# Hash-masked attention and a channel mix on one core: the fourth pair's values, three fillers, the last output's transpose and the order

## The chip, the core and the metric

The program runs on one core of a Trainium2 chip. The core has five engines with a queue of instructions each: PE (matmuls, with PEld for the loads of their stationary operand), ACT (exp, relu, tanh), DVE (vector work), POOL (more vector work) and SP, which here only issues DMAs. The metric is the time of one execution on the device in microseconds (us); less is better. The median of several executions is taken.

## The reference, cut to what matters

```python
q_bits = (einsum('bhsd,dk->bhsk', q, proj) > 0)          # 6 bits for each row; k_bits likewise
mask   = q_bucket[:, :, :, None] == k_bucket[:, :, None, :]
scores = where(mask, (q @ k.T) / sqrt(D), -1e9)
attn   = exp(scores - max);  attn /= (sum(attn) + 1e-9)
x      = (attn @ v)  laid out as (B, S, H * D)
x_prev = x shifted by one row (zeros ahead)
xk = mu_k * x + (1 - mu_k) * x_prev;   xr likewise with mu_r
out = sigmoid(xr @ w_r) * (relu(xk @ w_k) ** 2 @ w_v)
```

There are 4 batches, 8 heads, 768 rows, a head size of 64, a model size of 512 and an inner size of 1024. All inputs and the output are fp32.

## The kernel before

The heads are worked in 16 pairs, n = 0 to 15, four to a batch; behind a batch's last pair stands its channel mix (`add_moe`). For each pair:

- **Preparation.** q and k (`nat`) are split into a high and a low half of 64 columns each, both fp16, by DVE (L398 and L401, into `nh`), and turned by a DMA (L405) into `a`. Six more rows of `a` hold the hash bits: PE computes the projections (L427), DVE makes words of plus or minus a constant of their signs (L431, into `bx`), and POOL copies them into place with four instructions (L443, "the rows"), one for each of q and k and each head of the pair. With the bits as extra rows of the contraction, a score whose bits differ comes out so low that its exp vanishes, so there is no mask.
- **Scores.** Nine steps of 1024 columns: matmuls on PE (L544) into one of four PSUM buffers of two banks, then an exp on ACT (L548) into `pt`.
- **Values.** `pt` times the values `va` with a column of ones behind them, six groups of matmuls a pair (L571); DVE takes the reciprocal of the sums (`rc`) and multiplies (L589, into `ob`).
- **Rows without a partner.** A small share of the values' sum stands in for the mean. Pairs below `NUC` do it by a matmul (L566): POOL casts the values (L350), sums them together with the ones (L356, L359, L362, into `vsu`), and PE multiplies the sum by a matrix of 1e-12 (`tiny`) ahead of the pair's values. From pair `NUC` on, POOL sums the values alone (into `vs`), PE makes their mean in two layouts (L374 and L375, behind each other under the name mean), DVE subtracts it from the values (L380, two instructions a pair, into `va`) and keeps it by column (L387, into `mc`); the reciprocal then takes an add first (L584, L585 in place of L582), and the mean comes back at the mixing.
- **Turning the output.** `ob` is turned to `xt`, either on PE with six transposes (L599) and a copy by DVE (L602), for the pairs in `OT_PE`, or by a DMA that SP issues (L605). L612 makes its shifted neighbour; from pair `NUC` on, L609 writes the column ahead of the first row.
- **Mixing.** DVE takes the difference of neighbours (L630, `df`), and then, for `xk` and for `xr`, one instruction (L635) below `NUC`, two (L641, L644) from `NUC` on.

The channel mix of a batch multiplies `xk` by w_k (L659), takes the relu (ACT, L663) and the square (DVE, L666); multiplies `xr` by w_r (L679) and takes a tanh (ACT, L682); multiplies the squares by w_v (L692), and DVE combines the two (L699) for the store (L702). The weights are cast on POOL (L304). `warmb` ("fillers", L251) are pairs of matmuls on zeros, whose result nobody reads.

All of this is made as a list of operations, and a table, `ORDER`, gives the order in which they are issued, for all engines together; each engine takes its own in that order and waits for what the operation at its head needs. A second table, `BANKS`, gives each PSUM buffer its bank. So an operation that waits holds up everything behind it on its engine. Numbers behind a buffer's name tell its copies apart.

Of the kernel before, what the change touches and what calls it, by code (L numbers as in the profile page):

```python
# [128 lines left out]
def kernel(  # L129
# [30 lines left out]
    NUC = 4  # L160
# [6 lines left out]
    OT_PE = (0, 1, 2, 3, 15)  # L167
# [611 lines left out]
```

## Time and profile before

| | us |
|---|---|
| median of 3 runs | 243.16 (242.25 to 243.25) |
| the profiled execution | 242.0 |
| its span in the profile | 240.2 |
| PE busy | 234.1 |
| ACT busy | 181.9 |
| DVE busy | 179.8 |
| POOL busy | 99.7 |

The profile is of one execution. The span runs from its first instruction to its last; the profiled execution's own time is a little longer. "Busy" sums the instructions of an engine. PE and PEld overlap, and the ends of matmuls are modelled. In the rows of a timeline stand the start in us, the duration, the engine, the line, the operation and its tiles, and behind them, in brackets, how long the engine had been idle and what it waited for; x4 puts four in a row together.

### The profile page before, as it was taken

To read this page: it belongs to the slowest core of one execution; us is meant where nothing else is said; L and a number is where in the kernel's file an instruction comes from. 1 tells how busy PE (TensorE), PEld (TensorE's weight loads), DVE (VectorE), ACT (ScalarE), POOL (GpSimd) and SP (SyncE) were. 2 spreads that over 40 slices of the span, in tenths; PEclk is the share of its full clock that TensorE was granted. 3 is DMA by queue.
4 is the path that set the end of the run, shared out by engine and by line. 5 is a ranking of instruction groups with operands and counts; after the bars stand their busy time and mean duration, and the time that the engine had idled before them with its cause. 6 is when DMAs were issued, how large, how long until landed. Compare 5 with 4: busy or idle time off the path is not lost.

```text
span 240.2 us, 6251 instructions
## 1 busy us (share of the span) xinstructions
PE 234.1 (97%) x2515; PEld 147.8 (62%) x2532; DVE 179.8 (75%) x388; ACT 181.9 (76%) x242; POOL 99.7 (41%) x148
## 2 busy tenths in 40 slices
PE   8999999999999999999999999999999999999994
PEld 6985776776766565656456656665566564455442
DVE  3488789999998898989868896887167867348232
ACT  2699999999999999889779999677884640256320
POOL 4064979989934899438087302550000000000000
PEclk9999999999999999999999999999999999999999
DMA  6989999999999999988999989401500401210333
GB/s 225 304 222 274 232 242 260 279 197 362 279 253 284 273 213 294 249 302 206 276 163 241 249 177 234 136 0 26 173 0 3 120 3 44 87 46 1 131 135 131
DMA packets 72605, 44.00 MB, mean 183 GB/s; under 512 B 54912, under 2 KB 67584, under 8 KB 72576
## 3 DMA queue, kind: packets, MB, share of 16 engines
q1 hardware_dynamic: 72208, 43.20, 70.9%
q8 instruction: 20, 0.33, 0.6%
q10 hardware_dynamic: 368, 0.39, 0.5%
q14 instruction: 9, 0.07, 0.1%
HBM read 24.12 MB, written 6.29 MB: 127 GB/s over the span
## 4 chain that ended last, share of the span: by engine, by line
PE 92%; ACT 5%; issue 1%; DVE 0%
PE ps_all L544 25%; PE ps_all L692 17%; PE ps_all L659 16%; PE ps_all L571 14%; PE ps_all L679 8%; ACT pt L548 4%; PE ps_all L427 4%; PE ps_all L489 2%; PE ps_all L512 1%; PE ps_all L478 1%; ACT kr L663 1%; PE ps_all L251 1%; PE ps_all L246 1%; PE ps_all L599 1%; PE ps_all L566 1%
## 5 line engine op out<-in xcount | busy, mean ns | idle before, releaser
L548 ACT ACTIVATE pt<-ps_all 128x1024 bf16<-128x1024 f32 x144 | 138.4, 1041 | 10.9 <-PE ps_all L544 10.3
L544 PE MATMUL ps_all<-a 128*128 128x256 f16 (+1 forms) x384 | 79.2, 325 | 0.5 <-ACT pt L548 0.3
L443 POOL COPY a<-bx 6x384 f32<-6x384 f32 x56 | 38.9, 695 | 34.4 <-DVE bx L431 19.6
L544 PEld LDWEIGHTS <-a 128*128 128x128 f16 x384 | 34.0, 98 | 23.5 <-issue 4.6
L659 PE MATMUL ps_all<-xk,wk 128*128 128x384 bf16 x256 | 48.3, 326 | 0.1
L571 PEld LDWEIGHTS <-pt 128*128 128x128 bf16 x1152 | 42.5, 97 | 8.0 <-issue 0.5
L692 PE MATMUL ps_all<-wv,k 128*128 128x512 bf16 (+2 forms) x199 | 45.6, 362 | 0.5
L571 PE MATMUL ps_all<-va,pt 128*128 128x65 bf16 x1152 | 44.8, 193 | 0.0
L663 ACT ACTIVATE kr<-ps_all 128x384 bf16<-128x384 f32 x64 | 29.4, 491 | 16.0 <-PE ps_all L659 14.4
L659 PEld LDWEIGHTS <-wk 128*128 128x128 bf16 x256 | 24.2, 98 | 17.0 <-issue 0.6
L692 PEld LDWEIGHTS <-k 128*128 128x128 bf16 x208 | 19.3, 98 | 18.9 <-issue 0.3
L699 DVE SCALAR_TENSOR_TENSOR os<-rs,ps_all 128x512 f32<-128x512 f32 (+2 forms) x26 | 16.5, 643 | 19.0 <-PE ps_all L692 13.7
L682 ACT ACTIVATE rs<-ps_all 128x512 f32<-128x512 f32 x24 | 14.3, 602 | 20.5 <-PE ps_all L679 14.1
L666 DVE TENSOR_TENSOR k<-kr 128x384 bf16<-128x384 bf16 x64 | 23.2, 389 | 8.3 <-ACT kr L663 8.3
L401 DVE SCALAR_TENSOR_TENSOR nh<-nat,nh 128x1536 f16<-128x1536 f32 (+1 forms) x16 | 27.0, 1694 | 0.2
L679 PE MATMUL ps_all<-wr,xr 128*128 128x512 bf16 x88 | 23.2, 379 | 0.4
L356 POOL TENSOR_TENSOR vt<-vn 128x384 f32<-128x384 f32 x12 | 17.8, 1485 | 12.5 <-DMA vn<-in_v_dram 11.7
L589 DVE TENSOR_TENSOR ob<-ps_all,rc 128x384 bf16<-128x384 f32 x32 | 17.5, 553 | 1.4 <-DMA xt<-ob 0.8
L431 DVE TENSOR_SCALAR bx<-ps_all 128x768 uint16<-128x768 uint16 x14 | 13.4, 956 | 5.3 <-PE ps_all L427 4.7
L398 DVE TENSOR_SCALAR nh<-nat 128x1536 f16<-128x1536 f32 (+1 forms) x16 | 15.8, 985 | 0.3 <-PE ps_all L512 0.2
L679 PEld LDWEIGHTS <-xr 128*128 128x128 bf16 x96 | 9.0, 98 | 9.0
L380 DVE SCALAR_TENSOR_TENSOR va<-ps_all,vn 128x384 bf16<-128x384 f32 x24 | 12.7, 548 | 0.5 <-PE ps_all L375 0.2
(77 smaller groups left out, 188.9 us busy)
## 6 DMA issues: line engine op xcount, KB each, us to landing
vn<-in_v_dram SPq DMA_DIRECT2D x16, 384.0 KB, 5.1
out_dram<-os SPq DMA_DIRECT2D x23, 256.0 KB, 2.3
nat<-in_k_dram SPq DMA_DIRECT2D x15, 384.0 KB, 4.7
nat<-in_q_dram SPq DMA_DIRECT2D x15, 384.0 KB, 5.2
wst<-in_moe_w_k_dram SPq DMA_DIRECT2D x2, 512.0 KB, 7.0
wst<-in_moe_w_r_dram SPq DMA_DIRECT2D x2, 512.0 KB, 5.8
wst<-in_moe_w_v_dram SPq DMA_DIRECT2D x2, 512.0 KB, 4.4
k<-in_moe_w_k_dram SPq DMA_DIRECT2D x1, 512.0 KB, 4.4
```

Source lines behind the costliest of these rows:

```text
L356: e.tensor_tensor(out=vt[:, :, :, 0:E], in0=src[:, :, 0:3, 0:E], in1=src[:, :, 3:6, 0:E], op=ALU.add)
L401: nc.vector.scalar_tensor_tensor(out=nh[:, :, D:P], in0=nat.rearrange("p j (c d) -> p (j c) d", d=D), scalar=QS, in1=nh[:, :, 0:D], op0=AL ...
L443: nc.gpsimd.tensor_copy(side_a[side][n % NAQ][D : D + NB, j, :].bitcast(FP32), bx_t[sx][32 * i : 32 * i + NB, :].bitcast(FP32))
L544: nc.tensor.matmul(ps[:, lo - s * STEP : hi - s * STEP], side_a["k"][sa][:, j, jc * P : (jc + 1) * P], side_a["q"][sa][:, j, q0 : q0 + hi ...
L548: nc.scalar.activation(out=pt_t[sp][:, s * STEP : (s + 1) * STEP], in_=ps_t[plan.slot[nm]], func=AF.Exp, bias=EBIAS, scale=ESC)
L571: nc.tensor.matmul(oo[:, ic * 65 : ic * 65 + 65], pt_t[sp][:, o : o + P], va_t[sa][:, j, jc, 0 : D + 1], start=(not uc and ic == 0 and jc ...
L589: nc.vector.tensor_tensor(out=ob_t[so][:, :, j * D : (j + 1) * D], in0=oo[:, :, 0:D], in1=rc_t[sr][:, 1, :].unsqueeze(2).to_broadcast([P, ...
L659: nc.tensor.matmul(ps[:, 0:HALF], wk_sb[:, d, fc * P : (fc + 1) * P], xk_t[mx[d]][:, h * HALF : (h + 1) * HALF], start=(d == 0), stop=(d = ...
L663: nc.scalar.activation(out=kr_t[sk], in_=sm(nm)[:, 0:HALF], func=AF.Relu, scale=0.5 ** 0.5)
L666: nc.vector.tensor_tensor(out=k2_t[s2][:, h * HALF : (h + 1) * HALF], in0=kr_t[sk], in1=kr_t[sk], op=ALU.mult)
L679: nc.tensor.matmul(sm(nr), xr_t[mx[d]][:, c * P : (c + 1) * P], wr_sb[:, d, :], start=(d == 0), stop=(d == NDC - 1))
L692: nc.tensor.matmul(sm(nv)[:, x0:x1], k2_t[(b * NFC + fc) % NK2][:, c * P : (c + 1) * P], wv_sb[:, fc, x0:x1], start=(fc == 0), stop=(fc == ...
```

## The change

`NUC` goes from 4 to 3, so the fourth pair (n = 3) has its mean subtracted as the later pairs have. Five fillers are left of eight. Pair 15 is no longer in `OT_PE`, so its output is turned by a DMA. `ORDER` and `BANKS` are new tables.

```diff
 ORDER = [
...
-    0, 16, 2, 3, 4, 21, 5, 6, 7, 20, 8, 9, 10, 11, 37, 41, 33, 26, 1, 29, 28, 36, 30, 32, 40, 69, 72, 71, 70, 74, 73, 25, 43, 27, 31, 79,
...
+    0, 34, 66, 69, 38, 30, 23, 31, 16, 68, 71, 1, 26, 25, 2, 33, 3, 67, 70, 4, 27, 20, 29, 37, 74, 22, 5, 109, 6, 40, 24, 28, 7, 19, 44, 8,
...
 BANKS = [
-    2, 6, 2, 0, 4, 0, 0, 0, 0, 4, 4, 0, 3, 7, 1, 5, 4, 6, 1, 4, 5, 3, 4, 5, 2, 3, 4, 5, 4, 3, 0, 1, 2, 3, 0, 0, 0, 1, 7, 6, 6, 0, 2, 2, 2,
...
+    7, 5, 0, 0, 5, 6, 1, 2, 5, 0, 6, 1, 5, 1, 2, 4, 0, 0, 2, 7, 4, 6, 1, 2, 3, 2, 3, 2, 0, 3, 2, 0, 1, 1, 0, 5, 6, 6, 3, 1, 1, 2, 1, 0, 0,
...
-    NUC = 4
+    NUC = 3
...
-    OT_PE = (0, 1, 2, 3, 15)
+    OT_PE = (0, 1, 2, 3)
...
-    for i in range(8):
+    for i in range(5):
         def filler(i=i):
             for _ in range(2):
                 nc.tensor.matmul(sm(f"warmb{i}")[:, 0:256], wz[:, 0:P], wz[:, 0:256], start=True, stop=True)
```

On DVE, from the bits of pair 4 (`bx_67`) to those of pair 5 (`bx_68`), before:

```order
L431 TENSOR_SCALAR bx_67<-ps_all 128x768
L398 TENSOR_SCALAR nh_61<-nat_58 128x24x64
L630 TENSOR_TENSOR df_101<-xt_95 128x768
L401 SCALAR_TENSOR_TENSOR nh_61<-nat_58,nh_61 128x24x64
L582 RECIPROCAL rc_89<-ps_all 128x6
L589 TENSOR_TENSOR ob_92<-ps_all,rc_89 128x6x64
L582 RECIPROCAL rc_91<-ps_all 128x6
L589 TENSOR_TENSOR ob_93<-ps_all,rc_91 128x6x64
L635 SCALAR_TENSOR_TENSOR xr_111<-df_101,mur,xt_95 128x768
L602 COPY xt_96<-ps_all 128x768
L431 TENSOR_SCALAR bx_68<-ps_all 128x768
```

And the first half of the same place in the new order; `va_78` are the values of the fourth pair, and behind the last row shown stand eleven more ahead of `bx_68`: L585, L612, L589, two `va` of the next pair, `xr`, L584 and L585, `xk`, L589 and `mc`:

```order
L398 TENSOR_SCALAR nh_61<-nat_58 128x24x64
L431 TENSOR_SCALAR bx_67<-ps_all 128x768
L612 COPY xt_95<-xt_95 128x127
L380 SCALAR_TENSOR_TENSOR va_78<-ps_all,vn_69 128x6x64
L630 TENSOR_TENSOR df_101<-xt_95 128x768
L380 SCALAR_TENSOR_TENSOR va_78<-ps_all,vn_69 128x6x64
L582 RECIPROCAL rc_89<-ps_all 128x6
L387 TENSOR_SCALAR mc_84<-ps_all 128x1
L589 TENSOR_TENSOR ob_92<-ps_all,rc_89 128x6x64
L401 SCALAR_TENSOR_TENSOR nh_61<-nat_58,nh_61 128x24x64
L602 COPY xt_96<-ps_all 128x768
L584 TENSOR_SCALAR rc_91<-ps_all 128x6
```

One instruction, L398, has moved from behind the first bits to ahead of them, and 21 stand between the two bits where there were nine.

On POOL, from the rows of pair 3 (`a_66`) to the sums of pair 5, the new order (+) against the old (-); the first three sums taken away and put in are those of the fourth pair, and `a_64` are the rows of pair 5:

```order
 L443 COPY a_66<-bx_68 6x384 x4
-L356 TENSOR_TENSOR vt_72<-va_78 128x390
-L359 TENSOR_TENSOR vt_72<-vt_72 128x2x65
-L362 TENSOR_TENSOR vsu_76<-vt_72 128x130
+L356 TENSOR_TENSOR vt_72<-vn_69 128x6x64
+L359 TENSOR_TENSOR vt_72<-vt_72 128x2x64
+L362 TENSOR_TENSOR vs_74<-vt_72 128x128
 L356 TENSOR_TENSOR vt_72<-vn_70 128x6x64
 L443 COPY a_63<-bx_67 6x384 x4
```

The fourth pair's sums stay where they were, ahead of the rows of pair 4 (`a_63`), and take the values in fp32.

On SP, the last DMAs, before:

```order
L605 DMA_TRANSPOSE xt_94<-ob_92 128x6x128
L702 DMA out_dram<-os 128x512 x3
L605 DMA_TRANSPOSE xt_96<-ob_92 128x6x128
L702 DMA out_dram<-os 128x512 x13
L702 DMA out_dram<-os 128x128 x2
L702 DMA out_dram<-os 128x256
```

And in the new order, where `xt_97<-ob_93` is the output of pair 15:

```order
L605 DMA_TRANSPOSE xt_96<-ob_92 128x6x128
L702 DMA out_dram<-os 128x512 x3
L605 DMA_TRANSPOSE xt_97<-ob_93 128x6x128
L702 DMA out_dram<-os 128x512 x10
L702 DMA out_dram<-os 128x128 x2
L702 DMA out_dram<-os 128x512
L702 DMA out_dram<-os 128x256
```

The added DMA stands behind three stores, and one full store has moved to between the two small ones and the last.

116 rows, old and new, of tables (BANKS, ORDER) are left out of this document.

## The prediction

> **What bounds the kernel now.** The page first, for the share of each engine:
>
> ```profile
> span 240.2 us, 6251 instructions
> PE 234.1 (97%) x2515; PEld 147.8 (62%) x2532; DVE 179.8 (75%) x388; ACT 181.9 (76%) x242; POOL 99.7 (41%) x148
> ```
>
> The profiled execution took 242.0 us, 1.8 us more than its span; the median of the runs is 243.16 us, 1.16 us above it. I make the sum against 242.0 and carry that difference over to the median. A measurement of this kernel can tell about 0.5% from no change, 1.2 us.
>
> PE's 97% is an average, and its ends are modelled, so the next view is busy time by stage (the stretch, its length, then PE, PEld, DVE, ACT and POOL, each with its count):
>
> ```profile
> 20.00:45.00 25.00, 24.98 (x398) 17.37 (x396) 22.50 (x33) 25.00 (x29) 19.55 (x24) 1.00 1.08 258
> 45.00:58.00 13.00, 12.99 (x206) 8.76 (x203) 12.49 (x30) 12.79 (x15) 11.82 (x15) 1.00 1.13 271
> 58.00:85.00 27.00, 26.63 (x310) 17.08 (x309) 24.99 (x50) 26.51 (x39) 18.42 (x20) 1.00 1.14 281
> 120.00:200.00 80.00, 79.47 (x833) 48.23 (x842) 58.62 (x149) 59.85 (x80) 20.20 (x32) 1.00 0.49 115
> ```
>
> Two kernels in one. From 20 to 85 us ACT is idle for 0.7 us of 65 (25.00 + 12.79 + 26.51 busy), with DVE at 22.50 of 25 and 12.49 of 13 beside it: the exps pace this part, and PE is busy because its work is let in between them. From 120 us on ACT has 20 us to spare in 80 and PE 0.53: the matmuls pace that part. So a microsecond of PE work is worth a microsecond only well behind 85 us; ahead of that, what counts is whether the next exp finds its scores ready. The view of waits says the same: from 58 to 85 us ACT waited for the scores once.
>
> ```profile
> ACT pt L548 <- PE ps_all L544: 0.4, 1, 0.4
> ```
>
> **The change part by part.** *Fillers.* The head keeps five in both versions; the three that go stood in the middle of the scores. The timeline shows the first and the last of them, each with the weight load that follows:
>
> ```profile
> 26.84 0.21 PEld L251 LDWEIGHTS <-k 128*128 128x128 bf16 x2
> 27.06 0.51 PEld L571 LDWEIGHTS <-pt 128*128 128x128 bf16 x12
> ...
> 35.67 0.31 PEld L251 LDWEIGHTS <-k 128*128 128x128 bf16 x2
> 35.99 0.32 PEld L544 LDWEIGHTS <-a 128*128 128x128 f16 x3
> ```
>
> From a filler's start to the next work's is 0.22 and 0.32 us, so three are 0.7 to 1.0 us of PE. All lie where ACT was busy for 25.00 of 25.00: I count 0, and 0.9 in a rival.
>
> *Fourth pair.* What goes (the first three rows) and what comes, as groups with the mean of one in ns:
>
> ```profile
> L566 PE MATMUL ps_all<-vsu,tiny 128*128 128x390 bf16 x8 | 2.6, 330 | 0.0
> L350 POOL CAST va<-vn 128x768 bf16<-128x768 f32 x4 | 4.1, 1060 | 7.7 <-DMA vn<-in_v_dram 7.7
> L635 DVE SCALAR_TENSOR_TENSOR xk<-df,muk,xt 128x768 bf16<-128x768 bf16 x4 | 4.5, 1135 | 0.0
> L374 PE MATMUL ps_all<-vs,ones 128*128 128x128 bf16 x12 | 2.6, 220 | 0.0
> L380 DVE SCALAR_TENSOR_TENSOR va<-ps_all,vn 128x384 bf16<-128x384 f32 x24 | 12.7, 548 | 0.5 <-PE ps_all L375 0.2 <-issue 0.2
> L387 DVE TENSOR_SCALAR mc<-ps_all 128x1 f32<-128x1 f32 x12 | 1.7, 142 | 0.0
> L584 DVE TENSOR_SCALAR rc<-ps_all 128x6 f32<-128x6 f32 x24 | 3.8, 157 | 10.0 <-PE ps_all L571 9.5 <-ACT pt L548 0.6
> L641 DVE TENSOR_SCALAR tm<-df,muk,mc 128x768 f16<-128x768 bf16 x12 | 5.6, 470 | 0.1
> L644 DVE TENSOR_TENSOR xk<-tm,xt 128x768 bf16<-128x768 f16 x12 | 6.6, 553 | 0.1
> ```
>
> DVE gains 2 x 0.55 (va), 0.14 (mc), 0.14 (xz, another one-column instruction) and 2 x 0.16 (the adds of rc), 1.7 us, and loses 2 x (1.13 - 0.47 - 0.55) = 0.2: **+1.5 us on DVE**, nearly all ahead of 60 us. DVE was idle for 2.5 + 0.5 us from 20 to 58, so the work fits if it comes at the right places; I price it with the order below. POOL loses a cast of 1.06 us and gets wider sums for it, in an engine that is busy for 19.55 of 25: 0. PE loses two matmuls of 0.33 and gains one of 0.22 and a smaller one, at most 0.4 less, in the part that ACT paces: 0.
>
> There is a new wait. The fourth pair's sums (L362 ends them) now feed a matmul (L374) that stands in PE's queue right behind the fourth pair's bits (L427), with scores and the values' matmuls queued behind it.
>
> ```profile
> 39.64 0.83 PE L427 MATMUL ps_all<-a,p 128*32 128x512 f16 x16
> 39.93 0.42 POOL L362 TENSOR_TENSOR vsu<-vt 128x130 bf16<-128x130 f32 x1
> ```
>
> The sums ended at 40.35 us and those bits at 40.47, so PE finds them just ready: 0 to 0.5 us of PE, under ACT's stock of waiting scores, so 0 for the sum.
>
> *New order, pair 5.* Here I expect the cost. The rows of DVE, POOL and ACT around the bits of pair 4 (the first L431) and of pair 5 (the second), and two groups:
>
> ```profile
> 41.09 0.95 DVE L431 TENSOR_SCALAR bx<-ps_all 128x768 uint16<-128x768 uint16 x1
> 42.82 0.86 DVE L630 TENSOR_TENSOR df<-xt 128x768 bf16<-128x768 bf16 x1
> 42.15 4.41 POOL L443 COPY a<-bx 6x384 f32<-6x384 f32 x4
> 43.60 2.05 DVE L401 SCALAR_TENSOR_TENSOR nh<-nat,nh 128x1536 f16<-128x1536 f32 x1
> 47.89 0.55 DVE L602 COPY xt<-ps_all 128x768 bf16<-128x768 bf16 x1
> 48.81 0.96 DVE L431 TENSOR_SCALAR bx<-ps_all 128x768 uint16<-128x768 uint16 x1 [0.37 <-PE ps_all L427]
> 49.78 0.55 DVE L380 SCALAR_TENSOR_TENSOR va<-ps_all,vn 128x384 bf16<-128x384 f32 x1
> 49.89 2.40 POOL L443 COPY a<-bx 6x384 f32<-6x384 f32 x4 [0.57 <-POOL vt L356]
> 54.31 3.77 ACT L548 ACTIVATE pt<-ps_all 128x1024 bf16<-128x1024 f32 x4 [0.21 <-PE ps_all L544]
> L589 DVE TENSOR_TENSOR ob<-ps_all,rc 128x384 bf16<-128x384 f32 x32 | 17.5, 553 | 1.4 <-DMA xt<-ob 0.8
> L612 DVE COPY xt<-xt 128x127 bf16<-128x127 bf16 x16 | 3.5, 221 | 0.1
> ```
>
> Before, the second L431 began 7.72 us behind the first (48.81 - 41.09), 0.37 of it idle, so 7.35 us of work. In the new order L398 has gone ahead of the first, and between the two stand 21 instructions: 4 va, 3 ob, 5 of rc, df, lo, xt, xr, xk, 2 xs, 2 mc. By the rows: 4 x 0.55 + 3 x 0.55 + 5 x 0.16 + 0.86 + 2.05 + 0.55 + 2 x 1.13 + 2 x 0.22 + 2 x 0.14 = 11.1 us, and 12.0 with the first L431 itself. Instructions in a row start closer than they last (L431 to L380 above 0.97, but L630 to L401 0.78 for 0.86), which takes off some 6%: 11.3 us, **3.6 us more** than before, or 4.3 without that discount.
>
> The cover: the rows of pair 5 ended at 52.29 us (49.89 + 2.40) and its first exp began at 54.31, 2.0 us later, of which I give 0.7 to a score step and its hand-over. That leaves 1.3 us. And the new order asks first for a score step that needs two of the four rows only, 2 x 0.6 = 1.2 us more. Cover 2.5, delay 3.6: ACT waits **1.1 us**, with 0 and 2.3 as ends (none if the first L431 comes that much earlier than before, 2.3 if all four rows are needed after all).
>
> Does the added DVE work also hold up POOL's rows? Four of them took 2.40 us from 49.89 on while a `va` ran, and 4.41 us from 42.15 on beside L630 and L401. So I count the added `va` on DVE alone. Three POOL instructions more (two sums and a cast, about 1 us each by L350) now stand ahead of pair 5's rows; they run while the second L431 is late, so they cost nothing beyond that. [...]
>
> *Last output by a DMA.* Six transposes go from PE, in the part that PE paces. The weight loads of the last output's six and of the work behind them; the landing of DMA transposes in general; and two rows of the chain for the price of a group of matmuls:
>
> ```profile
> 201.35 0.54 PEld L599 LDWEIGHTS <-ob 128*128 128x128 bf16 x6
> 201.85 0.58 PEld L679 LDWEIGHTS <-xr 128*128 128x128 bf16 x4
> DMA to landing us min/median/max: 2.7/4.1/8.6
> 208.97 3.25 PE ps_all L659 x20
> 229.09 5.18 PE ps_all L692 x24
> ```
>
> From their first weight load to the next work's is **0.50 us**. [...] Is the landing covered? Behind the last matmul of pair 15 the new order has one L659 group (3.25 / 5 = 0.65 us) and ten of L692 or L679 (5.18 / 6 = 0.86 each), 9.3 us, before the last batch's first matmul on this output. The chain needs rc and ob (1 us), the landing, and xs, df, tm, xk with two L699 between (some 3.5 us): 7.2 us with the shortest landing, 8.6 with the median. On SP, only stores that are ready stand ahead of it. So it is covered: 0. If a landing took the longest, 8.6 us, the chain would be 13.1 and the cost 3.8.
>
> *The tail.* A full store now stands just ahead of the last one.
>
> ```profile
> out_dram<-os SPq DMA_DIRECT2D x23, 256.0 KB, 2.3
> ```
>
> It lands 2.3 us after its issue, and the last one is issued a matmul group behind it, so I count 0.
>
> **Sum:** -0.5 (transposes) + 1.1 (pair 5) = +0.6 us: 242.6 us profiled, 243.8 us as a median.
>
> **Rivals.** *A, PE's work counts everywhere.* If PE and ACT pace the first 85 us together, as 24.98 of 25.00 for PE lets one think, each filler is time: -0.9 for them, -0.4 for the fourth pair's matmuls, -0.5 for the transposes, and no wait at pair 5 because the scores get ahead: -1.8, and with ACT's 0.7 us of gaps -2.5 at most. 240.2 us profiled, 241.4 as a median (down to 240.7). For it: three of the four edits take work from the busiest engine. Against: ACT's 25.00.
>
> *B, pair 5 late in full.* The bank of PSUM that the fifth pair's bits leave is next taken by a matmul (L374) that stands ahead of more groups and the pair's first scores in PE's queue, so if the second L431 is late, PE stops too, and the stock of scores runs dry; with PE behind, the -0.5 is lost as well. Without the discount the delay is 4.3 and the wait 1.8. Pair 4 has the same pattern: its first exp comes one exp earlier in ACT's order, and a row beside DVE work took 1.1 us (4.41 / 4), so up to 1.1 for it. Price 1.1 to 3.4, typically +1.8: 243.8 us profiled, 245.0 as a median. It decides from a delay of the second L431 of over 4.2 us: 1.7 us of wait, 1.2 with the transposes off.
>
> [...]
>
> **How the numbers follow.** The forecast 0.33, A 0.32, B 0.33, C 0.02. Faster by over 0.5% is A, 0.32; within 0.5% is the forecast and C, 0.35; slower is B, 0.33. The likeliest case alone runs from 242.2 (no wait at pair 5, and half of the fillers counted) to 244.4. The range goes down to A, 240.8, and up to 245.6, which takes in two thirds of B.
>
> **What would show it.** Right: L431 of pair 5 starts at 51.5 us or later, ACT has a gap of 0.5 to 1.5 us before the first exp of pair 5, and from 85 us on PE has no new gap and six transposes fewer. A is right if ACT's counts up to 58 us (29 and 15) rise by one or more. B is right if ACT's busy time from 45 to 58 falls by over 1.5 us from 12.79. Wrong altogether would be a wait for `xt<-ob` before the last batch, or a gain or loss of over 1 us that arises behind 120 us.

## The result, and the profile after

| | before | after | ratio (95% interval) |
|---|---|---|---|
| median, us | 242.72 (17 runs) | 244.23 (17 runs) | 1.0059 (1.0044 to 1.0073) |
| the profiled execution, us | 242.0 | 243.6 | |
| its span, us | 240.2 | 241.7 | |

The change makes the kernel 1.5 us, or 0.6%, slower. The prediction was a median of 243.8 us, 0.6 us more than the one it started from, and it put its likeliest case within 0.5%. The sign was right and the size too small; 0.6% is also outside the 0.5% of its likeliest case.

The page after, its first two rows:

```profile
span 241.7 us, 6253 instructions
PE 234.4 (97%) x2520; PEld 147.4 (61%) x2520; DVE 183.4 (76%) x395; ACT 182.3 (75%) x242; POOL 97.5 (40%) x147
```

DVE has 3.6 us more (179.8 before), where the prediction counted 1.5; much of the rest is instructions that last longer (the 64 squares of L666 are busy for 24.7 us in place of 23.2). PE's total says nothing, since its work fell and its ends are modelled. Busy time by stage does, as before: the stretch, its length, then PE, PEld, DVE, ACT and POOL. The first fence is the head before, which the prediction didn't show; the second is after.

```profile
12.00:20.00 8.00, 8.00 (x76) 6.47 (x75) 6.62 (x12) 7.76 (x10) 5.47 (x8) 1.00 0.89 212
```

```profile
12.00:20.00 8.00, 7.88 (x75) 6.28 (x73) 5.69 (x12) 7.48 (x9) 4.93 (x7) 1.00 1.08 220
20.00:45.00 25.00, 24.20 (x365) 16.59 (x363) 23.10 (x38) 24.79 (x28) 18.16 (x24) 1.00 1.18 255
45.00:58.00 13.00, 12.31 (x217) 8.61 (x218) 12.83 (x29) 12.31 (x14) 10.17 (x13) 1.00 1.05 277
58.00:85.00 27.00, 25.83 (x303) 16.52 (x296) 24.49 (x48) 25.52 (x38) 17.53 (x20) 1.00 1.12 278
120.00:200.00 80.00, 80.00 (x869) 48.52 (x862) 59.95 (x146) 62.04 (x85) 21.85 (x33) 1.00 0.54 124
```

Read the ACT column up to 85 us, the fourth after the length. Against before it lost 0.28 us from 12 to 20 (7.76 to 7.48), 0.21 from 20 to 45 (25.00 to 24.79), 0.48 from 45 to 58 (12.79 to 12.31) and **0.99 from 58 to 85** (26.51 to 25.52): 1.96 us. Less the 0.5 us of the six transposes that is 1.5 us, against the 1.5 measured (and 1.6 between the two profiled executions). No run shows that 0.5 by itself, as the runs with the DMA below say, so the agreement holds to about half a microsecond. From 85 us on PE is busy in after for all of the 35 us to 120 and all of the 80 behind it, so no new gap arises there. Adding up how far apart PE's weight loads start, the two kernels differ by 0.1 us beyond their work from 105 us on; from 85 to 105 us they have different work in hand, and such a sum says nothing. So the loss arises where ACT paces, as the prediction had it, but half of it at a place that it didn't look at.

The waits of ACT's exps and of PE's score matmuls say where (engine, line, what it waited for: us in total, times, longest). After, 45 to 58 us, then 78 to 86 us:

```profile
PE ps_all L544 <- DVE ob L589: 0.5, 1, 0.5
ACT pt L548 <- PE ps_all L544: 0.4, 1, 0.4
```

```profile
ACT pt L548 <- PE ps_all L544: 1.2, 1, 1.2
PE ps_all L544 <- POOL a L443: 1.1, 1, 1.1
```

The second pair of rows is **pair 7**: PE waits for hash rows that POOL has not copied, and ACT starves behind it. Before, no wait of ACT is listed from 78 to 86 us. The timeline of POOL and of DVE there, after:

```profile
78.09 1.04 POOL L304 CAST wr<-wst 128x1024 bf16<-128x1024 f32 x1
79.20 3.30 POOL L443 COPY a<-bx 6x384 f32<-6x384 f32 x2
```

```profile
79.20 0.95 DVE L398 TENSOR_SCALAR nh<-nat 128x1536 f16<-128x1536 f32 x1
80.19 1.94 DVE L401 SCALAR_TENSOR_TENSOR nh<-nat,nh 128x1536 f16<-128x1536 f32 x1
```

In the new order a cast of weights (L304) stands between the four row copies of pair 7. It takes 1.04 us, and by its end DVE begins the halves of a later pair's q and k. The two copies left take 3.30 us, up to 82.50, and PE goes on at 82.55.

The first pair of rows, at 52 us, is not pair 5 but the end of pair 4. DVE, after:

```profile
49.82 1.84 DVE L635 SCALAR_TENSOR_TENSOR xk<-df,muk,xt 128x768 bf16<-128x768 bf16 x1
51.59 0.54 DVE L589 TENSOR_TENSOR ob<-ps_all,rc 128x384 bf16<-128x384 f32 x1
52.12 0.94 DVE L431 TENSOR_SCALAR bx<-ps_all 128x768 uint16<-128x768 uint16 x1
```

PE needs the PSUM bank that L589 frees and waits 0.5 us for it. L589 stands behind an `xk` that took 1.84 us beside another POOL cast (49.82 to 50.85 us). The second L431, whose delay the prediction priced, starts at 52.12, 3.3 us later than before, and the first exp of pair 5 at 55.33 (54.31 before). Directly ahead of that exp ACT was idle for 0.15 us, before for 0.21: the wait that the prediction priced isn't there.

### The profile page after: what moved, and what is told of

It is laid out like the page before. It is cut to its first block, busy times and chain, and to the rows that moved or that the text cites. A ratio compares the mean times of both kernels' runs of the same rounds, so it can differ in the third digit from the quotient of the medians.

```text
span 241.7 us, 6253 instructions
## 1 busy us (share of the span) xinstructions
PE 234.4 (97%) x2520; PEld 147.4 (61%) x2520; DVE 183.4 (76%) x395; ACT 182.3 (75%) x242; POOL 97.5 (40%) x147
## 4 chain that ended last, share of the span: by engine, by line
PE 85%; DVE 8%; issue 2%; POOL 2%; ACT 1%; DVEq 0%; POOLq 0%
PE ps_all L544 21%; PE ps_all L692 17%; PE ps_all L659 16%; PE ps_all L571 12%; PE ps_all L679 9%; PE ps_all L427 4%; PE ps_all L489 2%; POOL a L443 2%; DVE nh L401 1%; DVE bx L431 1%; PE ps_all L246 1%; PE ps_all L512 1%; DVE xr L635 1%; ACT pt L548 1%; PE ps_all L478 1%
## 5 line engine op out<-in xcount | busy, mean ns | idle before, releaser
L544 PE MATMUL ps_all<-a 128*128 128x512 f16 (+1 forms) x384 | 79.3, 325 | 2.5 <-POOL a L443 1.1
L692 PE MATMUL ps_all<-wv,k 128*128 128x512 bf16 (+2 forms) x208 | 46.7, 363 | 0.0
L571 PE MATMUL ps_all<-va,pt 128*128 128x65 bf16 x1152 | 44.3, 193 | 0.0
L666 DVE TENSOR_TENSOR k<-kr 128x384 bf16<-128x384 bf16 x64 | 24.7, 407 | 13.4 <-ACT kr L663 13.2
L699 DVE SCALAR_TENSOR_TENSOR os<-rs,ps_all 128x512 f32<-128x512 f32 (+2 forms) x26 | 16.6, 643 | 18.1 <-ACT rs L682 8.5
L401 DVE SCALAR_TENSOR_TENSOR nh<-nat,nh 128x1536 f16<-128x1536 f32 (+1 forms) x16 | 26.6, 1674 | 0.2
L679 PE MATMUL ps_all<-wr,xr 128*128 128x512 bf16 x96 | 24.3, 379 | 0.0
L589 DVE TENSOR_TENSOR ob<-ps_all,rc 128x384 bf16<-128x384 f32 x32 | 17.7, 554 | 0.6
L356 POOL TENSOR_TENSOR vt<-vn 128x384 f32<-128x384 f32 x13 | 16.2, 1249 | 1.3 <-DMA vn<-in_v_dram 0.4
L431 DVE TENSOR_SCALAR bx<-ps_all 128x768 uint16<-128x768 uint16 x14 | 13.4, 955 | 3.3 <-PE ps_all L427 2.9
L398 DVE TENSOR_SCALAR nh<-nat 128x1536 f16<-128x1536 f32 (+1 forms) x16 | 15.5, 972 | 0.0
L380 DVE SCALAR_TENSOR_TENSOR va<-ps_all,vn 128x384 bf16<-128x384 f32 x26 | 13.7, 548 | 0.8 <-PE ps_all L375 0.3
```

The source lines that it names most:

```text
L401: nc.vector.scalar_tensor_tensor(out=nh[:, :, D:P], in0=nat.rearrange("p j (c d) -> p (j c) d", d=D), scalar=QS, in1=nh[:, :, 0:D], op0=AL ...
L544: nc.tensor.matmul(ps[:, lo - s * STEP : hi - s * STEP], side_a["k"][sa][:, j, jc * P : (jc + 1) * P], side_a["q"][sa][:, j, q0 : q0 + hi ...
L571: nc.tensor.matmul(oo[:, ic * 65 : ic * 65 + 65], pt_t[sp][:, o : o + P], va_t[sa][:, j, jc, 0 : D + 1], start=(not uc and ic == 0 and jc ...
L589: nc.vector.tensor_tensor(out=ob_t[so][:, :, j * D : (j + 1) * D], in0=oo[:, :, 0:D], in1=rc_t[sr][:, 1, :].unsqueeze(2).to_broadcast([P, ...
L666: nc.vector.tensor_tensor(out=k2_t[s2][:, h * HALF : (h + 1) * HALF], in0=kr_t[sk], in1=kr_t[sk], op=ALU.mult)
L679: nc.tensor.matmul(sm(nr), xr_t[mx[d]][:, c * P : (c + 1) * P], wr_sb[:, d, :], start=(d == 0), stop=(d == NDC - 1))
```

## The experiments

Each change is given against the kernel named with it. Ratios are against the kernel before, with a 95% interval.

**Pair 7's rows.** After, with the cast moved behind the four copies (POOL):

```diff
-L443 COPY a_66<-bx_68 6x384 x2
+L443 COPY a_66<-bx_68 6x384 x4
 L304 CAST wr<-wst 128x1024
-L443 COPY a_66<-bx_68 6x384 x2
```

> The changed kernel with one POOL instruction moved: the cast of a weight (L304) that stood between the second and the third of the four row copies of pair 7 now stands behind the fourth. Theory (late rows: the time is lost where PE finds a row or a bank of PSUM not ready, and a stall ahead of 85 us reaches the end because PE has nothing to spare behind it): the third and fourth row run right behind the second, before DVE comes to L398 and L401, and take about 1.06 us in place of 3.30; PE's wait of 1.14 us for the row at 81 us and ACT's of 1.20 go, and the end comes 0.8 to 1.2 us earlier than in the changed kernel (about 243.2). Rival (the stall is absorbed later, since up to 85 us ACT has scores in stock and behind it other waits take its place): the wait goes, and the time stays within 0.3 us.

Measured: 243.26 us, ratio 1.003 (1.0013 to 1.0047): 0.7 us less than after by the ratios, 1.0 by the medians; the two intervals just overlap, but in the profile the wait is gone. POOL, and the stretch from 58 to 85 us:

```profile
77.42 2.18 POOL L443 COPY a<-bx 6x384 f32<-6x384 f32 x4 [7.81 <-DVE bx L431]
79.67 1.84 POOL L304 CAST wr<-wst 128x1024 bf16<-128x1024 f32 x1
```

```profile
58.00:85.00 27.00, 26.97 (x319) 17.33 (x318) 25.67 (x51) 26.72 (x39) 18.06 (x20) 1.00 1.09 277
```

All four rows are done at 79.60, before L398 begins; the cast takes the place beside DVE and nobody waits for it. ACT is busy for 26.72 us, 1.2 more than after. One cast, placed between four small copies, was about half of the loss.

**Pair 5.** After, with `xk` moved behind the bits (DVE), so that L431 comes earlier:

```diff
+L589 TENSOR_TENSOR ob_93<-ps_all,rc_90 128x6x64
+L387 TENSOR_SCALAR mc_85<-ps_all 128x1
+L431 TENSOR_SCALAR bx_68<-ps_all 128x768
 L635 SCALAR_TENSOR_TENSOR xk_105<-df_101,muk,xt_95 128x768
-L589 TENSOR_TENSOR ob_93<-ps_all,rc_90 128x6x64
-L387 TENSOR_SCALAR mc_85<-ps_all 128x1
-L431 TENSOR_SCALAR bx_68<-ps_all 128x768
```

> The changed kernel with one DVE instruction moved: xk of pair 1 (L635), which stood ahead of the bits of pair 5 (L431) and took 1.84 us beside a cast on POOL, now stands behind them. Theory (late rows): L431 of pair 5 starts about 1.1 us earlier than at 52.12, PE's wait of 0.8 us for the bank that L589 empties goes, and the end comes 0.5 to 1.0 us earlier than in the changed kernel. Rival (bits are late because of PE, which issues their matmuls at 50.18 us, so DVE's order is not what holds them): L431 starts no earlier than 51.0, the wait is shorter but a wait for rows replaces it, and the time moves by less than 0.3 us.

Measured: 244.82 us, ratio 1.009 (1.0069 to 1.011), 0.6 us slower than after. The bits came earlier, but the same `xk` now ran beside the rows:

```profile
51.31 0.96 DVE L431 TENSOR_SCALAR bx<-ps_all 128x768 uint16<-128x768 uint16 x1 [0.60 <-PE ps_all L427]
52.19 1.01 DVE L635 SCALAR_TENSOR_TENSOR xk<-df,muk,xt 128x768 bf16<-128x768 bf16 x1
```

```profile
52.40 3.06 POOL L443 COPY a<-bx 6x384 f32<-6x384 f32 x4 [1.38 <-issue]
```

```profile
45.00:58.00 13.00, 12.62 (x222) 9.00 (x223) 12.27 (x26) 12.56 (x14) 11.09 (x14) 1.00 1.05 285
58.00:85.00 27.00, 25.27 (x290) 16.05 (x282) 24.60 (x49) 24.84 (x37) 16.67 (x19) 1.00 1.10 271
```

Up to 58 us ACT gains 0.25 us (12.31 to 12.56), and by 85 it has lost 0.68 (25.52 to 24.84): the bits of pair 6 began at 59.62 in place of 58.75. No gain shows at the end. But the run doesn't test what earlier bits are worth, because the rows took 3.06 us against 2.38 in after and so ended at 55.46, when they had ended at 55.57 in after. The next edit keeps the bits late.

After, with the cast moved as above and L589 moved ahead of `xk` (DVE):

```diff
+L589 TENSOR_TENSOR ob_93<-ps_all,rc_90 128x6x64
 L635 SCALAR_TENSOR_TENSOR xk_105<-df_101,muk,xt_95 128x768
-L589 TENSOR_TENSOR ob_93<-ps_all,rc_90 128x6x64
```

> The changed kernel with the cast moved behind the row copies of pair 7 (0.97 us faster alone) and, on DVE, the multiplication that empties a bank of PSUM (L589, third pair's output) put ahead of xk (L635) in place of behind it; xk itself stays ahead of the bits of pair 5. Theory (two waits at pair 5: PE waited 0.8 us for this bank, DVE paces what stands behind it): the bank's wait goes and nothing is put off, 0.3 to 0.7 us faster than with the cast alone, at the kernel before or below it. Rival (as in the run where xk itself was put off: DVE has no slack there, so the wait comes back some us later): within 0.2 us of the run with the cast alone.

Measured: 242.80 us, ratio 1.0013 (0.9997 to 1.0029). The kernel can't be told from the one before. DVE, the first exp of pair 5, and the stages:

```profile
50.50 0.56 DVE L589 TENSOR_TENSOR ob<-ps_all,rc 128x384 bf16<-128x384 f32 x1
50.98 1.25 DVE L635 SCALAR_TENSOR_TENSOR xk<-df,muk,xt 128x768 bf16<-128x768 bf16 x1
...
52.22 0.94 DVE L431 TENSOR_SCALAR bx<-ps_all 128x768 uint16<-128x768 uint16 x1
...
55.43 6.77 ACT L548 ACTIVATE pt<-ps_all 128x1024 bf16<-128x1024 f32 x7 [0.20 <-PE ps_all L544]
```

```profile
45.00:58.00 13.00, 12.79 (x216) 8.93 (x218) 12.79 (x30) 12.67 (x15) 10.55 (x14) 1.00 1.06 281
58.00:85.00 27.00, 26.97 (x320) 17.40 (x312) 25.73 (x50) 26.72 (x39) 17.93 (x20) 1.00 1.08 271
```

L431 of pair 5 starts at 52.22, 3.4 us later than before. But the exps of this execution are late too: the first of pair 4 began at 46.77 us, 1.0 us later than before (45.74) and 0.57 later than in after (46.20), although up to there both have the same instructions (in the first 12 us ACT was busy for 5.00 us here, 5.57 in after). Against the exps the bits are thus 2.4 us later than before, and yet the first exp of pair 5 waited 0.20 us (0.21 before), and ACT is busy for 12.67 of 13 us (12.79 before). So that delay costs at most 0.1 us. Two instructions in their wrong places, a cast and an `xk`, made 1.1 us by the ratios of the 1.5 us lost. The share of the second, 0.4 us over the run with the cast alone, isn't clear of the noise by itself, since the two intervals overlap; what speaks for it is that PE no longer waits for L589.

**The fourth pair.** Before, with the edit of the fourth pair alone, `va` and `mc` behind the bits (DVE; what follows from `NUC = 3` on PE and POOL besides):

```diff
 L431 TENSOR_SCALAR bx_67<-ps_all 128x768
+L380 SCALAR_TENSOR_TENSOR va_78<-ps_all,vn_69 128x6x64 x2
+L387 TENSOR_SCALAR mc_84<-ps_all 128x1
 L398 TENSOR_SCALAR nh_61<-nat_58 128x24x64
```

> The kernel before with the fourth pair's edit alone: its values with their mean subtracted, all else in the old order (the mean's two matmuls stand behind the first group of values' matmuls that follows the fourth pair's bits, and the two L380 and L387 right behind the bits of pair 4 on DVE). Theory (the added DVE work itself costs only where it delays the rows): 1.2 us of DVE work is put ahead of L398 and L401 of pair 6 and of 8 instructions ahead of pair 5's bits, which come 0.9 to 1.3 us later than 48.81, with 1.3 to 2.5 us of cover: 0 to 0.5 us slower than before. Rival (DVE has nothing to spare up to 60 us, so its work is time): 1.2 to 1.5 us slower, which would be all of the loss.

Measured: 243.93 us, ratio 1.0055 (1.0038 to 1.0073): 1.3 us slower than before, so the theory's 0 to 0.5 falls. That is about the size that the rival gave to DVE's work as such, but the waits (41 to 54 us) name a mechanism:

```profile
PE ps_all L599 <- DVE ob L589: 1.2, 1, 1.2
ACT pt L548 <- PE ps_all L544: 1.0, 1, 1.0
```

L589 is behind L401 on DVE, which ran from 46.02 to 48.07; PE's transposes of that output waited for it, scores behind them, and ACT for these. The rows of pair 4 took 4.43 us, as before the change.

Before, with the edit and with DVE's order of after around those rows (L398 ahead of the bits, L401 behind both `va`, `mc`, `rc` and `ob`):

```diff
-L431 TENSOR_SCALAR bx_67<-ps_all 128x768
 L398 TENSOR_SCALAR nh_61<-nat_58 128x24x64
+L431 TENSOR_SCALAR bx_67<-ps_all 128x768
+L380 SCALAR_TENSOR_TENSOR va_78<-ps_all,vn_69 128x6x64
 L630 TENSOR_TENSOR df_101<-xt_95 128x768
+L380 SCALAR_TENSOR_TENSOR va_78<-ps_all,vn_69 128x6x64
+L387 TENSOR_SCALAR mc_84<-ps_all 128x1
+L582 RECIPROCAL rc_89<-ps_all 128x6
+L589 TENSOR_TENSOR ob_92<-ps_all,rc_89 128x6x64
 L401 SCALAR_TENSOR_TENSOR nh_61<-nat_58,nh_61 128x24x64
```

> The kernel before with the fourth pair's edit alone, as in the run that was 1.3 us slower, but with DVE's instructions around pair 4's rows in the order of the changed kernel: L398 ahead of the bits, and L401 behind the four row copies. Theory (a row copy on POOL that starts beside L398, L401 or L635 on DVE lasts until that has ended, 1.1 to 1.9 us in place of 0.50; so what counts is not DVE's added 1.5 us but where L401 falls): the four rows take about 2.4 us in place of 4.43, no wait at 48 us, and within 0.4 us of before. Rival (DVE's added work is time): 1.0 to 1.5 us slower than before, as when the instructions stood elsewhere.

Measured: 246.17 us, ratio 1.0152 (1.0132 to 1.0172). The rows did become short, but the mean's matmul, which has to be let in there, found no free bank. A row of the timeline, and the waits from 38 to 54 us:

```profile
44.52 2.38 POOL L443 COPY a<-bx 6x384 f32<-6x384 f32 x4 [1.80 <-issue]
```

```profile
PE ps_all L544 <- DVE ob L589: 1.4, 1, 1.4
PE ps_all L374 <- ACT pt L548: 1.1, 1, 1.1
PE ps_all L571 <- DVE mc L387: 0.5, 1, 0.5
```

For the rows the answer is clear, 2.38 us. The time decides nothing on the edit: the bank that I gave to the mean was held by a score step.

After, with the edit of the fourth pair undone (`NUC = 4`, the cast L350 ahead of its sums again; DVE):

```diff
 L431 TENSOR_SCALAR bx_67<-ps_all 128x768
 L612 COPY xt_95<-xt_95 128x127
-L380 SCALAR_TENSOR_TENSOR va_78<-ps_all,vn_69 128x6x64
 L630 TENSOR_TENSOR df_101<-xt_95 128x768
-L380 SCALAR_TENSOR_TENSOR va_78<-ps_all,vn_69 128x6x64
 L582 RECIPROCAL rc_89<-ps_all 128x6
-L387 TENSOR_SCALAR mc_84<-ps_all 128x1
 L589 TENSOR_TENSOR ob_92<-ps_all,rc_89 128x6x64
 L401 SCALAR_TENSOR_TENSOR nh_61<-nat_58,nh_61 128x24x64
```

> The changed kernel with the fourth pair's edit alone undone: its values get the ones and the matmul with 1e-12 again (a cast more on POOL ahead of its sums, two matmuls of 0.33 us more on PE, two L380 and four small instructions fewer on DVE), all else in the new order. Theory from the run with that edit alone in the old order (1.3 us slower): DVE has no time to spare up to 60 us and each microsecond of its work ahead of the bits of pair 5 delays them, so L431 of pair 5 starts about 1.3 us earlier than at 52.12, and the end comes 0.7 to 1.3 us earlier than in the changed kernel. Rival (that loss came from where the edit's instructions were put, and the new order was made around them): within 0.4 us of the changed kernel.

Measured: 246.27 us, ratio 1.0147 (1.0118 to 1.0177): 2.1 us *slower* than after, where a gain was expected. The expectation falls. The rows of pair 4 on POOL, two and two, and L401 on DVE in this kernel, and then all four and L401 in after:

```profile
42.84 1.25 POOL L443 COPY a<-bx 6x384 f32<-6x384 f32 x2
44.15 2.68 POOL L443 COPY a<-bx 6x384 f32<-6x384 f32 x2
...
44.16 1.75 DVE L401 SCALAR_TENSOR_TENSOR nh<-nat,nh 128x1536 f16<-128x1536 f32 x1
```

```profile
42.38 2.40 POOL L443 COPY a<-bx 6x384 f32<-6x384 f32 x4
...
44.43 1.96 DVE L401 SCALAR_TENSOR_TENSOR nh<-nat,nh 128x1536 f16<-128x1536 f32 x1
```

With `va` gone from between, L401 begins 1.3 us behind the start of the rows in place of 2.05. Two copies are done by then; the two that are left take 2.68 us, and the list of waits from 38 to 50 us has PE wait 1.8 us for the rows and ACT 1.7 us for PE. In the new order the added DVE work keeps L401 off the rows: edit and order belong together. (The cast that comes back on POOL is part of this; the rows start 0.46 us later.) Pair 4 is not all of it: against after, ACT is busy for 1.1 us less from 45 to 58 us (11.17) and for 0.9 less from 58 to 85 (24.65), where the rows of pair 6 take 4.89 us in place of 3.16. With the cast of pair 7 moved as well:

> The changed kernel with the fourth pair's edit undone, and the cast that stood between the row copies of pair 7 moved behind them. Theory (the two losses lie at different places and add up): 1.0 us (the cast, as measured alone) plus what the run with the edit undone alone gains, so 1.7 to 2.3 us faster than the changed kernel, at or below the kernel before. Rival (one stall hides the other: ACT's stock of scores, gained at pair 5, is lost again elsewhere): no more than 1.2 us faster than the changed kernel.

Measured: 245.87 us, ratio 1.0147 (1.0107 to 1.0187): 0.4 us less than without the move by the medians, nothing by the ratios, and slower than after, so neither side had it. The wait of pair 7 is gone (its rows take 2.18 us again), and the losses at pairs 4 and 6 stay; with an interval of 1 us on either side the run doesn't tell what the cast is worth here.

**The fillers.** Before, without the three that stood in the middle (PE):

```diff
-L251 LDWEIGHTS k_116
-L251 MATMUL ps_all<-k_116 128x256
-L251 LDWEIGHTS k_116
-L251 MATMUL ps_all<-k_116 128x256
 L571 LDWEIGHTS pt_86
```

> The kernel before without the three fillers that stand among the scores at 26.8, 35.0 and 35.7 us; nothing else is moved. Theory (the exps pace that part, so PE's work there is free): between 0.3 us faster and 0.3 us slower. Rival (PE's work counts everywhere): 0.7 to 1.0 us faster.

Measured: 242.51 us, ratio 0.9999 (0.9971 to 1.0028). A gain of 0.7 us would be 0.9971, the very end of the interval, and one of 0.9 us 0.9963: the full price isn't there, and 0 is the middle. In the profiled execution ACT has 12.40 us of work from 45 to 58 us in place of 12.79, so a smaller gain could hide behind a new wait.

**The last output by a DMA.** Before, with pair 15 turned by the DMA; I had put it ahead of a store on SP:

```diff
 L605 DMA_TRANSPOSE xt_96<-ob_92 128x6x128
+L605 DMA_TRANSPOSE xt_97<-ob_93 128x6x128
 L702 DMA out_dram<-os 128x512
```

> The kernel before with the last output (pair 15) turned by a DMA, issued right behind the DVE instruction that ends it, in place of PE's six transposes and DVE's copy; nothing else is moved. Theory (matmuls pace that part; the DMA lands about 2.75 us after its issue, at 202.2 us, as the copy ended at 202.9): 0.5 us faster, with no wait before L659 of the last batch. Rival 1 (the landing takes 4 us or more in the kernel): L659 waits, and the gain is gone. [...]

Measured: 244.22 us, ratio 1.007 (1.0045 to 1.0095), 1.6 us slower, which neither side expected. SP took its DMAs in turn, so the store waited for pair 15's output: issued at 190.16 us in the kernel before (the first fence), at 200.83 here. L699 waited for that store's buffer (the wait in brackets), and PE for the PSUM bank that L699 empties (the last row, from the list of waits):

```profile
190.16 24.01 SPq L702 DMA_DIRECT2D out_dram<-os  x5
```

```profile
189.10 11.68 SPq L605 DMA_TRANSPOSE xt<-ob  x2
200.83 5.25 SPq L702 DMA_DIRECT2D out_dram<-os  x4
...
203.26 0.69 DVE L699 SCALAR_TENSOR_TENSOR os<-rs,ps_all 128x512 f32<-128x512 f32 x1 [2.74 <-DMA out_dram<-os]
```

```profile
PE ps_all L692 <- DVE os L699: 1.2, 1, 1.2
```

The same, with the DMA one store later:

```diff
 L702 DMA out_dram<-os 128x512
+L605 DMA_TRANSPOSE xt_97<-ob_93 128x6x128
 L702 DMA out_dram<-os 128x512 x12
```

> The kernel before with pair 15's output turned by a DMA, as in the run that was 1.6 us slower, but with that DMA behind the store of the third batch row block (st1_3) in SP's queue and not ahead of it. In the slower run the store was issued at 200.83 us (190.16 before), because SP waited for pair 15's output, and DVE's L699 waited for the store's buffer until 203.26 and PE for L699's bank by 1.17 us. Theory (only the place in SP's queue was at fault): no such wait, 0.3 to 0.6 us faster than before. Rival (the landing of the DMA is the cost): L659 of the last batch still waits, and it is 0.5 us or more slower than before.

Measured: 242.79 us, ratio 1.0002 (0.9975 to 1.0029), no wait on a DMA from 195 us on. A gain of 0.5 us (0.9979) lies inside the interval, as does nothing; one of over 0.6 us (its lower end, 0.9975) doesn't.

After has no wait for the DMA of pair 15, but one of this kind for a store's buffer, up to 235.55 us (from its list for 195 to 241 us):

```profile
DVE os L699 <- DMA out_dram<-os: 3.5, 1, 3.5
```

PE doesn't wait for that L699, and the span ends 3.3 us behind PE's last matmul, 3.5 before, so it costs nothing that can be seen.

**The head.** ACT's exps waited for scores from 10 to 22 us, before and then after:

```profile
ACT pt L548 <- PE ps_all L544: 0.2, 1, 0.2
```

```profile
ACT pt L548 <- PE ps_all L544: 0.7, 2, 0.5
```

These 0.5 us more are all that ACT lost from 12 to 45 us (0.28 and 0.21 in the stages above).

After, with the first 20 us in the order of before:

```diff
 ORDER = [
-    0, 34, 66, 69, 38, 30, 23, 31, 16, 68, 71, 1, 26, 25, 2, 33, 3, 67, 70, 4, 27, 20, 29, 37, 74, 22, 5, 109, 6, 40, 24, 28, 7, 19, 44, 8,
+    0, 16, 2, 3, 4, 21, 5, 6, 7, 20, 8, 9, 10, 11, 37, 41, 33, 26, 1, 29, 28, 36, 30, 32, 40, 69, 72, 71, 70, 74, 73, 25, 43, 27, 31, 79,
...
```

> The changed kernel with the order of before for the first 20 us or so (all engines, to the end of the first pair's scores; its banks too), and the new order from there. In the new order ACT lost 0.71 and 0.33 us at two exps of the first pair, in the old one 0.43 at one. Theory (a wait of ACT ahead of 85 us reaches the end): 0.4 to 0.7 us earlier than the changed kernel. Rival (PE's work counts from the start, and PE idles there by about 0.25 us more only): 0.0 to 0.3 us earlier.

Measured: 246.06 us, ratio 1.0134 (1.0115 to 1.0152). The wait in the head went back to 0.2, and the seam between the two orders made another one, at 20 to 32 us:

```profile
ACT pt L548 <- PE ps_all L544: 1.9, 2, 1.7
PE ps_all L544 <- POOL a L443: 1.4, 1, 1.4
```

Again rows, those of pair 2, beside L398 and L401 (three of their copies took 4.25 us). So the run doesn't tell what the head costs. The second attempt put the seam at 30 us and kept both repairs, the cast and L589:

> The changed kernel with both repairs (the cast behind the row copies of pair 7, L589 ahead of xk at pair 5), and with the order of before for its first 30 us, up to the bits of pair 3, and no longer only for 20 us: there both orders have had the same instructions on DVE and POOL, so the seam should make no wait of its own, as the earlier seam did (1.87 us at an exp). Theory (each wait of ACT ahead of 85 us reaches the end): the wait of 1.04 us at two exps of the first pair becomes 0.43, and it is 0.3 to 0.7 us faster than with the two repairs alone, so 0.0 to 0.5 us faster than the kernel before. Rival (the first pair's exps are paced by PE's work in the head, which is the same): within 0.2 us of the run with the two repairs.

Measured: 243.43 us, ratio 1.0031 (1.0005 to 1.0057), 0.6 us more than without the old head by the medians and 0.4 by the ratios, whose intervals overlap. A gain was expected and doesn't show. A new wait stands at the seam again, from 28 to 38 us, where the run with the two repairs has none of ACT's:

```profile
PE ps_all L544 <- ACT pt L548: 0.8, 1, 0.8
ACT pt L548 <- PE ps_all L544: 0.7, 1, 0.7
```

So no version beat the kernel before, and what the new head costs at the end is not shown.

## Why the prediction was right and wrong, step by step

- **The sign: right by luck.** The forecast's loss was to come from a wait at pair 5, which isn't there: of its three signs L431 at 51.5 us or later came (52.12), and no new gap of PE from 85 us on, but not the gap of 0.5 to 1.5 us ahead of that pair's first exp (0.15). The measured loss came from pair 7, from a PSUM bank at pair 4's end and perhaps from the head, none of which the prediction had. By its size, 1.5 us, it lies nearer to B's 1.8 than to the forecast's 0.6, but not by B's mechanism: B's sign, a fall of over 1.5 us in ACT's time from 45 to 58 us, didn't come (0.48).
- **What bounds which part: right.** The time was lost where ACT paces, in steps in which an exp found its scores not ready, and from 85 us on PE has no new gap. Taking out three fillers gave nothing that could be measured, which speaks against rival A; ACT's counts up to 58 us fell by one each (28 and 14), where A asked for a rise.
- **Delay of the second L431, 3.6 us: too long.** It started 3.3 us later than before (48.81 to 52.12), but from the first L431 to the second it was 3.1: 10.81 us (41.31 to 52.12) in place of 7.72, where the prediction had 11.3. Instructions in a row start closer than the 6% that it took off: the durations in between, the slow `xk` with them, add up to 12.2, so it was 11%. And what counts is the delay against the exps, which were late themselves, by 0.46 us at pair 4's first (46.20 against 45.74) and by 0.41 more at the bank. That leaves 2.4 us, as in the run with both repairs.
- **Cover of 2.5 us: borne out as far as tested. Wait of 1.1 us at pair 5: wrong.** With 2.4 us of delay against the exps, the first exp of pair 5 waited no longer than before (0.15 and 0.20 us, 0.21 before). The longest such delay, 2.6 us, is in the last run shown under the head, and there it waited 0.29. The 0.48 us that ACT did lose from 45 to 58 us fell for the most part at pair 4's end, by way of the PSUM bank behind the slow `xk`. So of the two terms of this wait it was the delay that was mis-sized, and what ACT lost there came from another cause.
- **POOL's added instructions cost nothing: wrong.** The prediction looked at where POOL instructions stand around pair 5 only, and took POOL's idle time as cover. Of the three that it counted there, the cast at 49.82 us made `xk` 0.8 us longer, and L589 behind it late. The cast between pair 7's copies is on a path from L431 to ACT: 0.99 us, the largest single term, missed. An order of more than a thousand operations has to be looked through at every pair's rows, not at the first few.
- **`va` doesn't hold up the rows: right, and more than that.** In after they took 2.40 us at pair 4, against 4.41 before, and 3.99 without the two `va`. (Beside the slow rows the prediction named L630 and L401; L398 ran there too, 41.95 to 42.90.) The added work on DVE is a spacer there. The fourth pair's edit was priced as work (1.5 us on DVE). In this order taking it out costs 2.1 us, about half of it at pair 4; in the old order, at the one place tried where its mean found a free bank, it cost 1.3.
- **Fillers 0: right, to 0.7 us.** **Transposes -0.5: compatible, not shown**: the interval has 0.7 us on either side, and its middle is no gain. A higher price for a transpose, for which C stood, is shown by no run: the six took 0.50 us in the trace, and the run without them that has no wait for the DMA can't be told from the kernel before (1.0002).
- **DMA and tail 0: right, by its place.** After issues the DMA behind three stores and has no wait for it. One store earlier, tried in the old order, the same DMA cost 1.6 us: the prediction's remark that only ready stores stand ahead of it had the right concern, but the danger lay behind it, in the store that it would hold up.
- **The head: not looked at.** ACT lost 0.49 us at two exps up to 22 us. Whether that reaches the end stays open.

Sum: -0.5 for the transposes, 0.99 from 58 to 85 us (pair 7), 0.48 from 45 to 58 (pair 4's end), 0.49 in the head: +1.5, where the forecast had -0.5 and 1.1. The two in the middle were taken out by experiment; the first and the last were not shown by themselves.

## What to carry to other kernels

Where a short instruction feeds the engine that paces a stage, look at what stands between its parts in its queue, and at what starts on other engines beside them (here a row copy of 0.50 us on POOL took 1.92 beside L401 on DVE), for every tile that passes there. An edit that adds work can still keep a long instruction off such a place (four copies took 2.40 us with the two `va`, 3.99 without), so its price is not its duration; and an edit tried alone in the old order, or a piece of one order put on another, here mostly measured the new seam.

## What the runs showed of the hardware

The size of the trouble between POOL and DVE was not expected. A row copy takes 0.50 us when left alone, also beside `va` (0.50 at 77.53 us in after; four take 2.18 in the kernel with the cast moved; the four of 2.40 at pair 4 of after have one of 0.74 beside an L630). The two of pair 7 in after, one by one:

```profile
79.20 1.32 POOL L443 COPY a<-bx 6x384 f32<-6x384 f32 x1
...
80.58 1.92 POOL L443 COPY a<-bx 6x384 f32<-6x384 f32 x1
```

The first began with L398 (79.20 to 80.15) and ended 0.37 us behind it; the second began behind L401 (80.19 to 82.13) and ended 0.37 us behind that. Each got through once the DVE instruction was done. At pair 4 of after, where L401 began while the last copy was running (44.43, of rows that ended at 44.78), the rows lost nothing, and L401 took 1.96 us, against the 1.75 that it took where the copy was the late one (44.16 in the kernel with the edit undone). By the rows L398 reads one fp32 tensor (`nat`), L401 two (`nat` and `nh`), and `va` two (`ps_all` and `vn`); why a copy waits beside the first two and not beside `va`, no run here shows.

It goes the other way too: `xk` took 1.84 us in after, where POOL's cast (1.03 us) began with it at 49.82, 1.25 us where it began 0.6 us behind the cast, and 1.01 us where it began 0.2 us ahead of the rows, which then were the late ones (3.06). So in these rows, where the starts lie apart, the one that starts first isn't held up. Where they fall together, the rows don't say which was first: at 79.20 POOL was the late one, at 49.82 DVE. A cast that POOL has time for can cost DVE 0.8 us (1.84 against 1.01).
